# Softmax attention of one token over 8192 keys: longer chunks on VectorE, waits once per side, and the small steps between the pairs moved

## The chip, the core and the metric

The kernel runs on one NeuronCore of a Trainium2 chip. The core has five engines with their own instruction streams: TensorE (PE, matrix products), VectorE (DVE), ScalarE (ACT), GpSimd (POOL) and SyncE (SP, which here only issues transfers and waits), and 16 transfer (DMA) engines between device memory (HBM) and the on-chip memory (SBUF). Engines wait for one another by counting semaphores. The metric is the device time of one execution in microseconds; the median of three runs is taken.

## What is computed

One query row for each of 16 heads attends to 8192 keys of width 256, in bf16:

```python
B, H, Sq, Sk, D = 1, 16, 1, 8192, 256
def reference(q, k, v):
    scale = q.shape[-1] ** -0.5
    scores = jnp.einsum("bhqd,bhkd->bhqk", q, k) * scale
    p = _softmax(scores, axis=-1)
    return jnp.einsum("bhqk,bhkd->bhqd", p, v)
```

K and V are 67 MB each and every element is used once, so the kernel has to move 134 MB.

## The kernel before

**Tiling.** The 16 heads are taken as 8 pairs (`NP`). The K of a pair, "K h" below, fills 128 partitions with 64 for each head; a partition holds `J` = 128 keys, called columns, of 256 numbers each: 8.39 MB in all. V is laid out the same way. There are two buffers for K (`kbuf`, even and odd pairs) and one for V (`vbuf`). The columns of a pair are cut into two sides (`SIDES`) of 64.

**Scores.** Of the 64 columns of a side, GpSimd and ScalarE take the first 24 (`NPL`) and VectorE the other 40. GpSimd multiplies three columns at a time (a group, `GRP`) by the query and writes to `prod`, which holds two groups (L206 to L221); ScalarE adds each column up into `S` (L438 to L452). So GpSimd's group waits for the semaphore `sp`, with which ScalarE frees its half of `prod`, and ScalarE's for `tp`. A side has eight groups. VectorE multiplies and adds in one instruction per column (L243), in chunks of `CH` = 10 columns, four a side, and counts the chunks in `kd`. At the head of every chunk, and of every pair of groups on GpSimd, stand the same five waits: `k_waits` (the query of this pair has been copied, `qb`; K landed, `k0`, `k1`) and `side_wait` (`k6b`, `k7b`: the second sides of the last two Ks, which come as separate transfers).

**Softmax and V.** Behind each K VectorE takes the maximum over the columns (L263, semaphore `m`). TensorE turns it into a row (`turned`, L290), VectorE reduces that to one maximum per head (`xmax`, L231), TensorE spreads it (`spread`, L294), and ScalarE takes the exponentials (`expo`, L400 and L405, semaphore `ex`). TensorE then multiplies them with V, two columns at a time (`doubles`, L317), in a first half (semaphore `pa`) and a second, and adds up the sums (`total`, L305, semaphore `pr`). ScalarE copies the four strips of the result (`collect`, L419), called part rows here; TensorE adds these (`gather`, L339); VectorE takes the reciprocal of the sum (`recips`, L227), and ScalarE scales (`final`, L426).

**Where the small steps stand.** TensorE's loop does V of pair h-1 and then the maximum of pair h, in this order: wait `ex`, `doubles`, `total`, wait `m`, `turned`, wait `g`, `spread`, `keep_running` (a product with no use, L328), wait `cm`, `gather`, the query of pair h+2. VectorE and ScalarE do their small steps for earlier pairs between the columns of K h, at places written out by hand: `xmax` of pair h-1 behind the second chunk (20 columns) of side 0; `recips` of pair h-2 behind the first chunk of side 1; `expo` of pair h-1 behind group 4 of side 0 (the fifth), `collect` of pair h-2 behind group 6 of side 0, `final` of pair h-2 behind group 2 of side 1. Behind all 16 groups ScalarE copies the next query to `q_now` (`q_copy`, L396, semaphore `qb`).

**Transfers.** SyncE issues all of them in the order written out in `ORDER`, and stops at the first that can't go yet. K h waits until K h-2 is used up (`kd`, `tp`); V h until V h-1 is multiplied: a first half needs `pa`, a whole or a second half `pr`. The last Ks and Vs are cut: K6, K7 and V6 into halves ("k6", "k6+"), V7 at the columns 64, 92, 112 and 124 (`CUTS`). V7's first piece needs `pa` of V6, the later ones `pr` of V6. The columns of V7 from 92 on (`LAST_PAIRED`) are multiplied by 72 small products at the end (L382), and ScalarE and VectorE scale one half each of the last two rows (L472, L270).

```python
for kind, n, a, b, name in stream:
    if kind == "k" and n >= 2 and a == 0:
        sp.wait_ge(sem("kd"), (n - 1) * NC)
        sp.wait_ge(sem("tp"), (n - 1) * NG)
    elif kind == "v" and n >= 1 and a in (0, HJ):
        sp.wait_ge(*((sem("pa"), n) if b <= HJ else (sem("pr"), n + 2)))
```

## Time and profile before

| | us |
|---|---|
| median of three runs | 320.48 (320.45, 320.48, 321.91) |
| the profiled execution, whole time | 321.95 |
| its span, first to last instruction | 320.6 |
| VectorE busy | 229.2 (71%) |
| GpSimd busy | 210.8 (66%) |
| ScalarE busy | 195.3 (61%) |
| TensorE busy | 102.4 (32%) |
| moved from HBM | 134.23 MB, 419 GB/s over the span |

The profile is that of one execution. Its page has the busy time of each engine, the span in 40 slices with the busy tenths of each, the transfer queues, the chain of work that ended last, and the costliest groups of instructions. Other views list, in order of time, when instructions started, how long they took, and in brackets how long their engine had been idle and what ended that. A name with q behind it (SPq) is the engine's sequencer, which waits, branches and issues transfers. A group's line has the line of the code, the engine, the operation, the tile written and the ones read, the count, then the busy time in us, the mean of one in ns, and the idle time before it with its releaser.

### The profile page before, as it was taken

How to read it: one execution, taken by the hardware profiler on the slowest of the kernel's cores; microseconds unless marked ns; L12 is line 12 of the kernel's file. 1: busy time of each engine (PE TensorE's matmuls, PEld its weight loads, DVE VectorE, ACT ScalarE, POOL GpSimd, SP SyncE). 2: the span in 40 equal slices, each digit the busy share in tenths (PEclk: the TensorE clock that was granted, in tenths of full speed). 3: DMA queues.
4: the chain of work that ended last, by engine and by line, in shares of the span. 5: the costliest groups of instructions: out<-in, count | busy, mean ns of one | idle time of the engine just before them, and what ended most of it. 6: DMA issues, size and time to landing. Idle time of an engine off the chain costs nothing.

```text
span 320.6 us, 7869 instructions
## 1 busy us (share of the span) xinstructions
PE 102.4 (32%) x718; PEld 45.6 (14%) x718; DVE 229.2 (71%) x1305; ACT 195.3 (61%) x840; POOL 210.8 (66%) x146
## 2 busy tenths in 40 slices
PE   0000000037002570049102570027502104835678
PEld 0000000013000230014000230003200002412335
DVE  0008888688868888788878886788878886888810
ACT  2005766586656874777737873487757874788631
POOL 3008885879858685858658781769858785878400
PEclk9999999999655597557855596556955555978779
DMA  9999999999999999999999999999999999999994
GB/s 394 393 393 523 393 393 507 409 393 482 401 409 409 491 393 417 393 393 515 401 393 499 417 393 491 425 393 425 425 421 429 482 433 393 384 405 454 433 360 202
DMA packets 3353, 134.27 MB, mean 419 GB/s; under 512 B 374, under 2 KB 406, under 8 KB 662
## 3 DMA queue, kind: packets, MB, share of 16 engines
q1 hardware_dynamic: 3332, 134.23, 97.9%
q8 instruction: 1, 0.02, 0.0%
q14 instruction: 2, 0.02, 0.0%
q10 hardware_dynamic: 18, 0.01, 0.0%
HBM read 134.23 MB, written 0.01 MB: 419 GB/s over the span
## 4 chain that ended last, share of the span: by engine, by line
DMA 31%; DVE 25%; DVEq 21%; issue 18%; PE 3%; ACT 1%; SPq 0%
DMA kbuf<-in_k_dram 31%; DVE kbuf L243 25%; DVEq L243 13%; DVEq L156 2%; PE acc L317 2%; DVEq L238 2%; DVEq L152 1%; DVEq L157 1%; PE ob L382 1%; ACT E L405 0%; DVEq L254 0%; DVEq L257 0%; DVEq L237 0%; DVEq L153 0%; DVE small L231 0%
## 5 line engine op out<-in xcount | busy, mean ns | idle before, releaser
L243 DVE SCALAR_TENSOR_TENSOR kbuf<-kbuf,qrow x640 | 223.8, 417 | 75.0 <-issue 72.5
L214 POOL TENSOR_TENSOR prod<-kbuf,q_now 128x768 f32<-128x768 bf16 x128 | 208.0, 1639 | 88.0 <-issue 41.6
L445 ACT ACTIVATE prod<-prod x384 | 155.4, 405 | 105.7 <-POOL prod L214 92.0
L317 PE MATMUL acc<-vbuf,E 128*64 128x512 bf16 x494 | 70.0, 452 | 25.1 <-DMA vbuf<-in_v_dram 23.3
L445 ACT ACTIVATION_READ_ACCUMULATOR prod<-prod x384 | 71.6, 186 | 0.0
L243 DVE DVE_READ_ACCUMULATOR kbuf<-kbuf,qrow x640 | 52.9, 83 | 0.0
L317 PEld LDWEIGHTS acc<-vbuf,E 128*64 128x64 bf16 x494 | 31.9, 130 | 61.9 <-DMA vbuf<-in_v_dram 25.2
L290 PE MATMUL mx<-ident,small 128*1 128x128 f32 x16 | 4.3, 364 | 105.7 <-DVE small L263 105.7
L294 PE MATMUL mx<-small 1*64 1x1 f32 x32 | 2.8, 239 | 58.1 <-DVE small L231 58.1
L290 PEld LDWEIGHTS mx<-ident,small 128*1 128x1 f32 x16 | 0.7, 80 | 106.7 <-DVE small L263 106.7
L339 PE MATMUL ob<-comb,small 98*2 98x128 f32 x64 | 7.6, 386 | 24.8 <-ACT comb L419 24.8
L405 ACT ACTIVATE E<-S,negb 64x128 bf16 (+1 forms) x16 | 13.8, 865 | 1.4 <-ACT negb L400 1.2
L328 PE MATMUL spare<-ident 128*128 128x512 f32 x16 | 13.8, 955 | 0.0
L294 PEld LDWEIGHTS mx<-small 1*64 1x64 f32 x32 | 2.1, 183 | 61.7 <-DVE small L231 61.7
L419 ACT ACTIVATE comb<-acc 98x512 f32<-98x512 f32 x8 | 4.6, 579 | 6.4 <-PE tot L305 6.4
L339 PEld LDWEIGHTS ob<-comb,small 98*2 98x2 f32 x64 | 2.8, 101 | 36.0 <-ACT comb L419 34.2
L405 ACT ACTIVATION_READ_ACCUMULATOR E<-S,negb 64x1 f32 x16 | 7.9, 494 | 0.0
L227 DVE RECIPROCAL small<-tot 34x1 f32 (+1 forms) x8 | 1.2, 154 | 8.8 <-PE tot L305 8.8
L426 ACT ACTIVATE qo<-ob,small 2x128 f32 (+1 forms) x14 | 4.9, 353 | 0.1
L400 ACT ACTIVATE negb<-mx 128x1 f32<-128x1 f32 x8 | 1.3, 161 | 5.6 <-PE mx L294 5.6
L263 DVE TENSOR_REDUCE small<-S 128x1 f32 x8 | 2.3, 286 | 2.5 <-DVE kbuf L243 2.5
L281 PE MATMUL qrow<-qo,which 2*128 (+1 forms) x8 | 2.9, 393 | 2.9 <-DMA qo<-in_q_dram 2.6
(25 smaller groups left out, 22.0 us busy)
## 6 DMA issues: line engine op xcount, KB each, us to landing
kbuf<-in_k_dram SPq DMA_DIRECT2D x4, 4096.0 KB, 36.6
vbuf<-in_v_dram SPq DMA_DIRECT2D x3, 4096.0 KB, 14.4
vbuf<-in_v_dram SPq DMA_DIRECT2D x1, 1792.0 KB, 9.1
vbuf<-in_v_dram SPq DMA_DIRECT2D x1, 1280.0 KB, 11.9
vbuf<-in_v_dram SPq DMA_DIRECT2D x1, 768.0 KB, 13.3
vbuf<-in_v_dram SPq DMA_DIRECT2D x1, 256.0 KB, 13.5
kbuf<-in_k_dram SPq DMA_DIRECT2D x6, 31.9
vbuf<-in_v_dram SPq DMA_DIRECT2D x6, 28.8
```

What stands on the lines that cost most here:

```text
L156: e.wait_ge(sem("k6b"), (h * SIDES + s + 3) // (NP * SIDES) * 16 + 16)
L214: pool.tensor_tensor(out=prod[:, b * GRP * D : (b + 1) * GRP * D].rearrange("p (b d) -> p b d", b=GRP), in0=kbuf[:, ds(par * (J * D) + s * ...
L238: with dve.Fori(0, SC) as c:
L243: ins = dve.scalar_tensor_tensor(out=col, in0=col, scalar=SCALE, in1=qrow[:, ds(par * 512, D)], op0=ALU.mult, op1=ALU.mult, accum_out=S[:, ...
L290: pe.matmul(mx[0:1, 0:P], lhsT=m[:, :], rhs=ident[:, :], start=True, stop=True).then_inc(sem("mT"), 1)
L294: ins = pe.matmul(sm[n * HP : (n + 1) * HP, :], lhsT=ones[0:1, :].to_broadcast([1, HP]), rhs=g[:, n : n + 1], start=True, stop=True,)
L317: ins = pe.matmul(acc[at : at + STRIP, :], lhsT=E[:, x : x + STRIP], rhs=vbuf[:, j * D : (j + 2) * D], start=(j < 4), stop=(j >= J - 4), s ...
L328: pe.matmul(spare[:, :].rearrange("p (b x) -> p b x", x=P), lhsT=ident[:, :], rhs=ident[:, :].rearrange("p (b x) -> p b x", b=1).to_broadc ...
L339: ins = pe.matmul(ob[row : row + 2, 0:HW], lhsT=sel[:, 2 * n : 2 * n + 2], rhs=comb[:, n * D + a : n * D + a + HW], start=(n == 0), stop=( ...
L405: ins = act.activation(out=E[rows, 0 : 2 * J].rearrange("p (b two i t) -> p b i two t", b=J // BLK, two=2, t=2)[:, :, :, :, x], in_=S[rows ...
L426: ins = act.activation(out=qo[:, ds(i * D + a, HW)], in_=ob[row : row + 2, 0:HW], func=ACT.Copy, scale=recip[row : row + 2, ds(i, 1)],)
L445: ins = act.activation(out=part, in_=part, func=ACT.Copy, scale=SCALE, accum_out=S[:, ds(par * J + s * HJ + i * GRP + b, 1)],)
```

## The change

`CH` becomes 20, so VectorE has two chunks a side. The five waits are made once per side, ahead of the inner loop, on VectorE and on GpSimd, followed by a `nop` that counts up a semaphore `turn` that nobody waits for. The small steps move: `late` is 0 for pairs 0 to 6 and 1 for the last, and they stand in side `late`. On VectorE `xmax` and `recips` both come behind its first chunk (20 columns). On ScalarE `collect` comes behind group 1, `expo` behind group 3 and `final` behind group 6.

```diff
-CH = 10
+CH = 20
...
                 with pool.Fori(0, SIDES) as s:
+                    k_waits(pool, h)
+                    side_wait(pool, h, s)
+                    pool.nop().then_inc(sem("turn"), 1)
                     with pool.Fori(0, SG // 2) as i:
-                        k_waits(pool, h)
-                        side_wait(pool, h, s)
                         for b in range(2):
...
+                late = dve.snap(h // LAST)
                 with dve.Fori(0, SIDES) as s:
+                    k_waits(dve, h)
+                    side_wait(dve, h, s)
+                    dve.nop().then_inc(sem("turn"), 1)
                     with dve.Fori(0, SC) as c:
-                        k_waits(dve, h)
-                        side_wait(dve, h, s)
                         for b in range(CH):
...
                         ins.then_inc(sem("kd"), 1)
-                        with dve.If(s == 0):
-                            with dve.If(c == 1):
+                        with dve.If(c == 0):
+                            with dve.If(s == late):
                                 with dve.If(h > 0):
                                     xmax(h, 1)
-                        with dve.If(s == 1):
-                            with dve.If(c == 0):
                                 with dve.If(h > 1):
                                     recips(h, 2)
...
+                late = act.snap(h // LAST)
...
                         ins.then_inc(sem("sp"), 1)
-                        with act.If(s == 0):
-                            with act.If(i == 4):
+                        with act.If(s == late):
+                            with act.If(i == 1):
+                                with act.If(h > 1):
+                                    collect(h, 2)
+                            with act.If(i == 3):
                                 with act.If(h > 0):
                                     expo(h, 1)
                             with act.If(i == 6):
-                                with act.If(h > 1):
-                                    collect(h, 2)
-                        with act.If(s == 1):
-                            with act.If(i == 2):
                                 with act.If(h > 1):
                                     final(h, 2)
```

## The prediction

> **What bounds the kernel now.** I read the page's busy tenths first, then SyncE's waits, then the chain of waits and the timelines of single engines at the places that these name. K h and V h are the K and V of pair h; a full one is 8.39 MB.

> ```profile
> span 320.6 us, 7869 instructions
> DMA  9999999999999999999999999999999999999994
> SPq L137 <- PE tot L305: 113.0, 6, 27.5
> SPq L126 <- POOL prod L214: 105.2, 6, 50.9
> SPq L137 <- PE acc L317: 53.4, 2, 38.9
> 0.81 21.88 DMA kbuf<-in_k_dram
> 162.53 38.12 DMA kbuf<-in_k_dram
> ```

> The transfer engines are busy in every slice but the last, so the time is that of the stream of bytes, plus whatever empties the queue, plus the work behind the last byte. SyncE's rows say what can empty it: an issue of V stands behind TensorE (L305, or L317 for a half), one of K behind GpSimd and VectorE. No engine's speed counts by itself; what counts is whether it lets SyncE issue before the queue is dry.

> ```profile
> 268.54 9.74 PE L317 MATMUL acc<-vbuf,E 128*64 128x512 bf16 x64 [15.50 <-DMA vbuf<-in_v_dram]
> 287.96 5.12 PE L317 MATMUL acc<-vbuf,E 128*64 128x512 bf16 x32 [1.16 <-DMA vbuf<-in_v_dram]
> 297.68 5.33 PE L317 MATMUL acc<-vbuf,E 128*64 128x512 bf16 x32 [4.60 <-DMA vbuf<-in_v_dram]
> 78.33 0.33 SPq L137 DMA_DIRECT2D vbuf<-in_v_dram  x1
> 118.56 0.33 SPq L137 DMA_DIRECT2D vbuf<-in_v_dram  x1
> 153.25 0.33 SPq L137 DMA_DIRECT2D vbuf<-in_v_dram  x1
> ...
> 274.86 3.81 SPq L137 DMA_DIRECT2D vbuf<-in_v_dram  x2
> 293.12 0.33 SPq L137 DMA_DIRECT2D vbuf<-in_v_dram  x1
> 317.88 0.32 SPq L144 DMA_DIRECT2D out_dram<-qo  x1
> ```

> TensorE started V5, the front half of V6 and its back half as they landed. Between the first two lie two halves, 19.4 us; between the last two one half, 9.7 us. That is the stream undisturbed. K0 landed at 22.7 (0.81 + 21.88), so 2.5 us go to the start of a stream. At this rate K5, nine transfers on, would be in at 22.7 + 9 x 19.4 = 197.3; the chain has it at 162.53 + 38.12 = 200.65. So 3.35 us were lost before K5. The issues show where: V1 went out at 78.33, 2.6 us before K2 was due (80.9), and V2 at 118.56, 1.1 us before K3 was due (100.3 + 19.4 = 119.7). V3 at 153.25 had over 5 us. A start takes 2.5 us, so these two were late. The last bytes were in at 317.88 (L144 waits for them).

> **The change part by part.**

> VectorE's chunks:

> ```profile
> L243 DVE SCALAR_TENSOR_TENSOR kbuf<-kbuf,qrow x640 | 223.8, 417 | 75.0 <-issue 72.5
> 92.39 0.29 DVE L263 TENSOR_REDUCE small<-S 128x1 f32 x1 [0.31 <-DVE kbuf L243]
> 94.50 0.42 DVE L243 SCALAR_TENSOR_TENSOR kbuf<-kbuf,qrow  x1 [1.83 <-issue]
> 94.85 0.08 DVE L243 DVE_READ_ACCUMULATOR kbuf<-kbuf,qrow  x1
> 95.19 0.08 DVE L243 DVE_READ_ACCUMULATOR kbuf<-kbuf,qrow  x1
> L214 POOL TENSOR_TENSOR prod<-kbuf,q_now 128x768 f32<-128x768 bf16 x128 | 208.0, 1639 | 88.0 <-issue 41.6
> 201.62 3.24 POOL L214 TENSOR_TENSOR prod<-kbuf,q_now 128x768 f32<-128x768 bf16 x2 [7.87 <-DMA kbuf<-in_k_dram]
> 235.69 3.23 POOL L214 TENSOR_TENSOR prod<-kbuf,q_now 128x768 f32<-128x768 bf16 x2 [3.35 <-issue]
> 239.42 1.64 POOL L214 TENSOR_TENSOR prod<-kbuf,q_now 128x768 f32<-128x768 bf16 x1 [0.50 <-ACT prod L445]
> 269.74 3.23 POOL L214 TENSOR_TENSOR prod<-kbuf,q_now 128x768 f32<-128x768 bf16 x2 [3.35 <-issue]
> ```

> A column takes 0.34 us (94.85 to 95.19), a K's 80 take 27.3. The end of a K takes 0.31 + 0.29 + 1.83 = 2.4. VectorE's idle time put down to issue is 72.5 us: 24 before the first K, 1.83 at each of six starts, and the other 37 over 56 gaps between chunks, about 0.7 each. Seven gaps of a K become three. The two that disappear into a side cost from nothing to 0.7 each, the gap between sides 0.9; with 0.4 for the maximum and the reciprocal a K is 27.3 + 2.4 + 0.9 + 0.4 + (0 to 1.4), 31 to 32.4 us, where it was about 35. I take 31.5: 20 columns give the sequencer 6.8 us to run ahead.

> What is late next is the GpSimd-ScalarE loop. VectorE waits at each K for ScalarE's copy of q, made behind all 16 groups, and GpSimd's K starts stand 34.07 and 34.05 us apart (201.62, 235.69, 269.74). So a K costs 34.05, not 31.5.

> GpSimd's own waits: the gap before a pair of multiplies is 0.50 and its releaser is ScalarE's sum, two groups back. The five waits before it stand inside that time, while the second multiply runs, so moving them out gives nothing; a pair stays at 3.74 (235.69 to 239.42). If they were the gap, up to 0.34 a pair would go; I take 0 and keep 0.34 for a rival. The two added nops per K cost a semaphore update each, 0 to 0.3 us, hidden by the same loop on GpSimd and by the spare 2.5 us on VectorE.

> The moved steps in K1 to K6:

> ```profile
> 108.12 1.02 PE L339 MATMUL ob<-comb,small 98*2 98x128 f32 x8 [3.35 <-ACT comb L419]
> 109.40 9.10 PE L317 MATMUL acc<-vbuf,E 128*64 128x512 bf16 x64
> ```

> TensorE began V1 only behind the gather of V0's part rows, held 3.35 us by ScalarE's collect. The collect now comes ahead of the exponentials, and these one group (1.87 us) sooner. V1 then starts some 6 us earlier, at about 103.4, and V2's issue moves from 118.56 to about 112.5. For K1 only the exponentials move, some 1.9 us: V1's issue goes to about 76.5. Both are then ahead by more than the 2.5 us start, and K5 lands at 197.3. The collect and the reciprocal wait for the total of V(h-2); behind them stand ScalarE's groups and VectorE's next chunk. That total is out before K h starts (V1's at 118.5, and K3 is not in before 119.7), so nothing is held. None of these steps issues a transfer.

> The last K, which decides:

> ```profile
> 25.84 0.42 ACT L445 ACTIVATE prod<-prod  x1 [22.45 <-POOL prod L214]
> 46.13 0.42 ACT L445 ACTIVATE prod<-prod  x1 [0.29 <-issue]
> 280.47 0.17 ACT L400 ACTIVATE negb<-mx 128x1 f32<-128x1 f32 x1
> 281.70 0.87 ACT L405 ACTIVATE E<-S,negb 64x128 bf16 x1
> 285.15 0.57 ACT L419 ACTIVATE comb<-acc 98x512 f32<-98x512 f32 x1
> 316.81 2.18 PE L382 MATMUL ob<-vbuf,E 128*2 128x128 bf16 x72
> 319.04 0.36 ACT L472 ACTIVATE qo<-ob,small 2x128 bf16<-2x128 f32 x1 [3.01 <-PE ob L382]
> ```

> Pair 6's exponentials now stand in K7 behind 12 groups of ScalarE instead of 5. TensorE's V6 waits for them; V7's front half (L128, L137) waits for V6's front half; nothing else is left to issue. Before, they ended at 282.57, V6's front landed at 287.96, and V7 went out at 293.12, with V6's back half on its way until 297.68. Now:
> - K5 in at 197.3, GpSimd starts 0.97 later (201.62 - 200.65): 198.3. Two Ks of 34.05: K7 at 266.4.
> - In K0, where nothing interrupts, GpSimd starts at 23.8, ScalarE's first group at 25.84, its 12th at 46.13, ending 1.2 later: 23.5 us behind GpSimd's start. So 289.9; the collect of 0.57, partly in slack, adds 0.3: 290.2. The maximum is there: from a start near 267, VectorE's 60 columns take 20.5 and the gaps 1 to 2, about 289.
> - The exponentials, 280.47 to 282.57, 2.1; TensorE starts at 292.4.
> - V6's front half at the row of 287.96, 5.12: V7's front half is issued at 297.6 instead of 293.12.
> - V6's back half is in at 197.3 + 5 x 19.4 = 294.3. So the **queue runs dry** for about 5.5 us. From an empty queue a half takes 9.7 + 2.5 = 12.2: 309.8. (V6's front, issued at 274.86 as the queue ran out, took 13.1: the upper end.)
> - The last 64 columns: 9.7 undisturbed, 10.5 the other way (317.88 - 297.68 less 9.7). I take 10.0: 319.8.
> - From the last byte: 8 of the 72 small matmuls (72 take 2.2) 0.25, then as before from TensorE's end at 319.04 to the span's end at 320.6, 1.55. Span 321.6.

> Pair 7's exponentials follow V6's end, some 3.5 us behind 297.6, by a maximum and 2.1 us of ScalarE, about 305: before V7's front lands, so they cost nothing. Outside the span the execution has 321.95 - 320.6 = 1.35; so **323.0 us**, 1.0 above the profiled execution and 2.5 above the median of the three runs. Two of those were 1.5 shorter than the profiled execution, which fits a chance number of late issues; since the sum leaves none before K5, I carry no part of that difference over.

> The clock of TensorE in V6's front half:

> ```profile
> 290.00:291.00 1.00, 1.00 (x8) 0.42 (x6) 1.00 (x9) 0.95 (x6) 1.00 (x1) 0.51 0.45 197
> 291.00:292.00 1.00, 1.00 (x12) 0.53 (x10) 1.00 (x9) 0.20 (x1) 1.00 (x2) 1.00 1.14 492
> ```

> The windows view gives the granted clock behind the five engines, before the transfers' share: 0.51, then 1.00. V6's front half, from 287.96, so ran its first 3 us at half clock. At full clock it would cost what V5's back half did: V6 was issued at V5's middle, 274.86, and V5 ended at 278.28 (268.54 + 9.74), 3.4 us. [...]

> **The rivals.**
> [...]
> - **The hoisted waits do shorten GpSimd's pair** (the other side, faster): from 3.74 to 3.4. K6 and K7 up to group 12 are 14 pairs, 4.8 us; V7 goes out at 292.8, the dry stretch nearly closes, 305.0 + 10.0 + 1.8 + 1.35 = 318.2. It decides from 0.19 a pair (2.5 / 14). Against: the releaser is ScalarE.
> - **The chunks don't do what they say** (slower): the gaps stay, a K costs 35.2, K7 starts 2.3 later: 325.3. Or V1 or V2 is still late, up to 3.35 more: 326.3.

> **How the numbers follow.** Forecast 0.55, full clock 0.18, shorter pair 0.15, gaps stay 0.12. About 0.5%, 1.6 us, is what a measurement here can tell from no change: 318.9 to 322.1. Slower takes the forecast and the last rival, 0.66; same 0.20; faster 0.14. The range is 319.5 to 325.3: the forecast's bounds (13.1 for the half, 10.5 for the columns, 1.4 more) reach 325, the warm clock lies inside, most of the shorter pair and of a late V1 outside.

> **What would show it.** V2's issue near 112 and K5 used at about 198; K7 from GpSimd at 266; pair 6's exponentials ending at 292, V6's front following at once; SyncE's first V7 issue near 297.6 and the transfers' share falling before it. The prediction is wrong if that issue comes before 292, if GpSimd's gap falls under 0.3, or if K5 still lands at 200.

## The result, and the profile after

| | before | after |
|---|---|---|
| median, us | 320.72 (320.45 to 321.91, now 4 runs) | 325.51 (324.83 to 326.57, 4 runs) |
| profiled execution, us | 321.95 | 326.57 |
| its span, us | 320.6 | 325.2 |

After takes 1.0145 times as long as before (95% interval 1.0106 to 1.0184): slower, with the sign and by the mechanism of the forecast, but 2.5 us above its 323.0 and 0.2 above the end of its range. The profiled execution was the slowest of the four. The ratios, here and below, leave out executions more than 1.5% above the fastest of their kernel.

The page's rows of the span, of the busy share of the transfer engines in 40 slices and of the bytes they moved, after:

```profile
span 325.2 us, 7165 instructions
DMA  9899899899899999999998999989999999992994
GB/s 388 387 459 444 387 508 395 387 508 395 387 508 395 419 476 395 451 443 395 500 403 387 508 395 419 476 387 419 423 451 480 419 391 423 423 431 69 400 396 187
```

Before, only the last slice was short of a 9. Now there is a hole in the 37th slice (69 GB/s, 293 to 301 us). The 8s ahead of it cost nothing that the trace shows: K5 landed at 197.65 all the same (157.17 + 40.48 in the chain), against 197.3 for the undisturbed stream. Windows of 2 us in that stretch of after (busy time of TensorE, its weight loads, VectorE, ScalarE, GpSimd; then the granted clock of TensorE, the transfers' share, GB/s):

```profile
294.00:296.00 2.00, 1.69 (x8) 0.74 (x10) 2.00 (x13) 1.85 (x10) 0.13 (x2) 0.50 0.00 0
296.00:298.00 2.00, 2.00 (x16) 0.95 (x14) 1.49 (x10) 1.00 (x7) 2.00 (x2) 0.67 0.00 0
298.00:300.00 2.00, 2.00 (x22) 1.09 (x20) 0.00 (x0) 1.97 (x8) 1.15 (x1) 1.00 0.00 0
```

For six whole microseconds nothing moves, while TensorE, ScalarE and VectorE work. What starts the stream again is SyncE's issue of V7. SyncE's timeline of after:

```profile
76.99 0.33 SPq L137 DMA_DIRECT2D vbuf<-in_v_dram  x1
111.54 0.33 SPq L137 DMA_DIRECT2D vbuf<-in_v_dram  x1
...
299.46 0.33 SPq L137 DMA_DIRECT2D vbuf<-in_v_dram  x1
...
321.84 0.32 SPq L144 DMA_DIRECT2D out_dram<-qo  x1
```

V1 and V2 go out earlier than before, as meant; V7 goes out 6.3 us later (299.46 against 293.12). The chain to it, from the timelines of ScalarE and TensorE:

```profile
292.10 0.15 ACT L401 ACTIVATE negb<-mx 128x1 f32<-128x1 f32 x1
293.31 0.86 ACT L406 ACTIVATE E<-S,negb 64x128 bf16 x1
```

```profile
290.65 0.38 PE L295 MATMUL mx<-small 1*64 1x1 f32 x4 [15.49 <-DVE small L232]
290.96 2.08 PE L329 MATMUL spare<-ident 128*128 128x512 f32 x2
292.97 1.02 PE L340 MATMUL ob<-comb,small 98*2 98x128 f32 x8
294.31 8.56 PE L318 MATMUL acc<-vbuf,E 128*64 128x512 bf16 x64 [0.33 <-ACT E L406]
...
311.98 8.01 PE L318 MATMUL acc<-vbuf,E 128*64 128x512 bf16 x46 [6.52 <-DMA vbuf<-in_v_dram]
...
321.44 2.18 PE L383 MATMUL ob<-vbuf,E 128*2 128x128 bf16 x72
```

The spread of pair 6's maximum is out in time (290.65), so the exponentials stand only behind ScalarE's groups: they run from 292.10 (280.47 before). TensorE waits for them, no longer for V6, which had long landed, and its front half ends where V7 is issued. V7's products start 12.5 us behind that issue. GpSimd's starts of K5, K6 and K7, which set when ScalarE reaches its 12th group, and the next pair of K5:

```profile
198.77 3.22 POOL L215 TENSOR_TENSOR prod<-kbuf,q_now 128x768 f32<-128x768 bf16 x2 [6.84 <-issue]
202.50 1.64 POOL L215 TENSOR_TENSOR prod<-kbuf,q_now 128x768 f32<-128x768 bf16 x1 [0.50 <-ACT prod L447]
...
233.59 3.23 POOL L215 TENSOR_TENSOR prod<-kbuf,q_now 128x768 f32<-128x768 bf16 x2 [3.51 <-issue]
...
268.40 3.24 POOL L215 TENSOR_TENSOR prod<-kbuf,q_now 128x768 f32<-128x768 bf16 x2 [3.51 <-issue]
```

K5 starts 2.85 us earlier than before. But a K now takes 34.82 where it took 34.06 (the mean of 34.07 and 34.05), so K7 starts only 1.3 earlier. VectorE's two rows among the costliest groups:

```profile
L246 DVE SCALAR_TENSOR_TENSOR kbuf<-kbuf,qrow x640 | 220.3, 413 | 46.2 <-issue 46.2
...
L264 DVE TENSOR_REDUCE small<-S 128x1 f32 x8 | 2.3, 286 | 31.8 <-ACT prod L447 31.8
```

VectorE did get faster: its idle time put down to issue fell from 72.5 to 46.2 us. What it gained it spends waiting for ScalarE, 31.8 us over the eight maxima.

### The profile page after: what moved, and what is told of

The parts are those of the page before. It is cut to its first block, busy times and chain, and to the rows that moved or that the text cites. A ratio compares the mean times of both kernels' runs of the same rounds, so it can differ in the third digit from the quotient of the medians.

```text
span 325.2 us, 7165 instructions
## 1 busy us (share of the span) xinstructions
PE 103.9 (32%) x718; PEld 46.6 (14%) x718; DVE 224.9 (69%) x1305; ACT 195.3 (60%) x840; POOL 210.1 (65%) x146
## 4 chain that ended last, share of the span: by engine, by line
POOL 23%; DMA 23%; ACT 16%; issue 15%; ACTq 12%; PE 5%; POOLq 5%; SPq 0%
POOL prod L215 23%; DMA kbuf<-in_k_dram 19%; ACT prod L447 14%; ACTq L447 8%; PE acc L318 4%; DMA vbuf<-in_v_dram 4%; POOLq L215 3%; ACTq L443 2%; ACT E L406 1%; PE ob L383 1%; ACT q_now L397 1%; ACTq L456 1%; POOLq L212 0%; ACTq L459 0%; POOLq L214 0%
## 5 line engine op out<-in xcount | busy, mean ns | idle before, releaser
L215 POOL TENSOR_TENSOR prod<-kbuf,q_now 128x768 f32<-128x768 bf16 x128 | 207.3, 1639 | 87.0 <-issue 46.6
L246 DVE SCALAR_TENSOR_TENSOR kbuf<-kbuf,qrow x640 | 220.3, 413 | 46.2 <-issue 46.2
L318 PE MATMUL acc<-vbuf,E 128*64 128x512 bf16 x494 | 71.2, 459 | 44.5 <-DMA vbuf<-in_v_dram 42.4
L246 DVE DVE_READ_ACCUMULATOR kbuf<-kbuf,qrow x640 | 51.0, 80 | 0.0
L318 PEld LDWEIGHTS acc<-vbuf,E 128*64 128x64 bf16 x494 | 32.8, 132 | 81.5 <-DMA vbuf<-in_v_dram 43.8
L295 PE MATMUL mx<-small 1*64 1x1 f32 x32 | 2.9, 245 | 70.5 <-DVE small L232 70.5
L264 DVE TENSOR_REDUCE small<-S 128x1 f32 x8 | 2.3, 286 | 31.8 <-ACT prod L447 31.8
L329 PE MATMUL spare<-ident 128*128 128x512 f32 x16 | 14.7, 1018 | 0.0
L295 PEld LDWEIGHTS mx<-small 1*64 1x64 f32 x32 | 2.2, 191 | 74.1 <-DVE small L232 74.1
L340 PE MATMUL ob<-comb,small 98*2 98x128 f32 x64 | 7.3, 373 | 0.0
L340 PEld LDWEIGHTS ob<-comb,small 98*2 98x2 f32 x64 | 2.7, 99 | 11.5 <-issue 9.8
L329 PEld LDWEIGHTS spare<-ident 128*128 128x128 f32 x16 | 3.6, 282 | 0.1
```

Source lines behind the costliest of these rows:

```text
L215: pool.tensor_tensor(out=prod[:, b * GRP * D : (b + 1) * GRP * D].rearrange("p (b d) -> p b d", b=GRP), in0=kbuf[:, ds(par * (J * D) + s * ...
L246: ins = dve.scalar_tensor_tensor(out=col, in0=col, scalar=SCALE, in1=qrow[:, ds(par * 512, D)], op0=ALU.mult, op1=ALU.mult, accum_out=S[:, ...
L295: ins = pe.matmul(sm[n * HP : (n + 1) * HP, :], lhsT=ones[0:1, :].to_broadcast([1, HP]), rhs=g[:, n : n + 1], start=True, stop=True,)
L318: ins = pe.matmul(acc[at : at + STRIP, :], lhsT=E[:, x : x + STRIP], rhs=vbuf[:, j * D : (j + 2) * D], start=(j < 4), stop=(j >= J - 4), s ...
L329: pe.matmul(spare[:, :].rearrange("p (b x) -> p b x", x=P), lhsT=ident[:, :], rhs=ident[:, :].rearrange("p (b x) -> p b x", b=1).to_broadc ...
L340: ins = pe.matmul(ob[row : row + 2, 0:HW], lhsT=sel[:, 2 * n : 2 * n + 2], rhs=comb[:, n * D + a : n * D + a + HW], start=(n == 0), stop=( ...
```

## The experiments

The theory is that of the prediction: the late steps of the last K hold V7's issue until the queue is dry. Its rivals: the hoisted waits or the longer chunks cost the time; the tests and moved steps slow ScalarE in every K; TensorE's half clock costs the time. Each run is compared with before on its own chip.

| run | median, us (range, runs) | before beside it | ratio (95%) |
|---|---|---|---|
| e1 no late steps | 320.54 (319.69–322.05, 12) | 321.30 | 0.9969 (0.9944–0.9995) |
| e2 late steps alone | 341.20 (340.54–341.74, 4) | 321.30 | 1.0600 (1.0542–1.0658) |
| e3 chunks, waits alone | 320.57 (318.19–324.09, 12) | 321.30 | 0.9961 (0.9930–0.9991) |
| e4 `final` at its old place | 326.56 (325.34–328.12, 4) | 321.30 | 1.0166 (1.0109–1.0223) |
| e5 idle products before V7 | 327.27 (327.06–328.57, 4) | 321.13 | 1.0205 (1.0176–1.0233) |
| e6 V7 into K6's buffer | 319.69 (319.07–320.57, 12) | 321.13 | 0.9965 (0.9949–0.9980) |
| e7 chunks and waits undone | 327.01 (325.94–328.34, 4) | 321.13 | 1.0176 (1.0145–1.0207) |
| e8 idle products, two places | 326.44 (325.61–326.68, 4) | 321.31 | 1.0159 (1.0137–1.0182) |
| e9 the change again | 326.08 (325.27–326.64, 4) | 321.31 | 1.0145 (1.0116–1.0174) |
| e10 more, moved | 326.73 (325.78–327.09, 5) | 321.04 | 1.0179 (1.0166–1.0193) |
| e11 the change again | 325.36 (324.66–325.58, 4) | 321.04 | 1.0125 (1.0107–1.0142) |
| e12 idle products without a gap | 324.50 (324.09–324.91, 7) | 321.23 | 1.0089 (1.0055–1.0123) |

### e1: the change without its late steps

```diff
-                        with act.If(s == late):
+                        with act.If(s == 0):
...
-                            with dve.If(s == late):
+                            with dve.If(s == 0):
```

The two lines that compute `late` go as well.

> The changed kernel with late = 0 for every pair: the small steps stand in side 0 of the last K too. Theory (the late exponentials of pair 6 run the transfer queue dry): ScalarE's collect waits in K7 for V5's total at about 275, the exponentials of pair 6 end at about 281 to 282 instead of 294.2, V6's front half starts when it lands (about 286), V7's first piece is issued at about 291 instead of 299.5, the queue does not run dry, and the time falls by 5 us or more, to 318.5 to 320.5. Rival (the longer chunks, the waits per side or the early steps of K1 to K6 cost the time): it stays near 325.

The whole loss is gone: 320.5 us, 5 below the change. SyncE's issue of V7 (five issues grouped in one row) and TensorE's V6, in the timelines of e1:

```profile
291.35 11.77 SPq L137 DMA_DIRECT2D vbuf<-in_v_dram  x5
```

```profile
285.27 6.04 PE L317 MATMUL acc<-vbuf,E 128*64 128x512 bf16 x32 [7.64 <-DMA vbuf<-in_v_dram]
```

TensorE waits for V6 itself again, and V7 goes out at 291.35, 8.1 us before the change's. The page's transfer row of e1 has a 9 in every slice but the last. So the late side of the last K costs the 5 us, and the rest of the change gains a little at most (0.9969). The edit also takes the test against `late` out of every K, and K7 starts 0.6 us earlier for it (267.81 against 268.40); that is the smaller part of the 8.1.

### e2: the late steps alone, on the kernel before

```diff
-                        with act.If(s == 0):
-                            with act.If(i == 4):
+                        with act.If(s == late):
+                            with act.If(i == 4 - late):
...
-                            with act.If(i == 6):
+                            with act.If(i == 6 - 2 * late):
...
-                            with act.If(i == 2):
+                            with act.If(i == 2 + 4 * late):
```

VectorE's two steps move to side 1 of the last K in the same way, `recips` by `c == late`.

> The kernel before with one thing changed: in the last K the maximum, the reciprocal, the exponentials, the part rows and the final scaling stand in side 1 (behind its 20th column, and behind groups 3, 4 and 6). Theory: GpSimd starts K7 at 269.7 as before, ScalarE's 12th group ends 23.7 later, the exponentials end at about 295.6, V7's first piece is issued at about 301 instead of 293.1, and the time is 327 to 328.5, above the changed kernel, since K5 lands late as well. Rival (something else in the change costs the time): 320 to 321.5.

A miss: this edit confounds itself, and 341 us is far above the 5 us of e1. A group's first sum on ScalarE, first of the change, then of e2; GpSimd's starts and SyncE's V7 in e2:

```profile
202.58 0.42 ACT L447 ACTIVATE prod<-prod  x1 [0.48 <-issue]
```

```profile
209.36 0.42 ACT L447 ACTIVATE prod<-prod  x1 [0.84 <-issue]
```

```profile
205.18 3.23 POOL L214 TENSOR_TENSOR prod<-kbuf,q_now 128x768 f32<-128x768 bf16 x2 [3.57 <-issue]
...
241.70 3.23 POOL L214 TENSOR_TENSOR prod<-kbuf,q_now 128x768 f32<-128x768 bf16 x2 [3.58 <-DMA kbuf<-in_k_dram]
```

```profile
315.57 5.29 SPq L137 DMA_DIRECT2D vbuf<-in_v_dram  x5
```

In the side that holds the late steps the gap before a group's first sum is 0.84 us ahead of the second group (209.36) and 0.83 ahead of the third, both put down to issue; ahead of the second the change has 0.48. A K takes 36.5 us (205.18 to 241.70), K7 starts at 278.20, and V7 goes out at 315.57. That computing the places from `late` is the cause is an inference; it was not tried alone. There is a second difference: `collect` stands behind the exponentials here and not ahead of them, TensorE's gather waits for it, and V6's front half starts at 309.32, 31.1 us behind GpSimd's K7, where the change needs 25.9 (268.40 to 294.31). So this run can't separate the late steps from either; e1 does.

### e3: the chunks and the waits alone

```diff
-CH = 10
+CH = 20
...
+                    k_waits(pool, h)
+                    side_wait(pool, h, s)
+                    pool.nop().then_inc(sem("turn"), 1)
```

The same on VectorE; the small steps stay where they were, `xmax` behind the first chunk of 20.

> The kernel before with the chunks of 20 and the waits per side, the small steps left where they were (the maximum behind 20 columns of side 0, the reciprocal now behind 20 columns of side 1). Theory: VectorE's K falls from 35.2 to about 28 us of work plus a wait for ScalarE, GpSimd's loop stays at 34.1 to 34.3 a K, so the K before the last does not start earlier by more than what V1's issue gains; VectorE's last K ends with ScalarE's at about 302 instead of 305.2; 319 to 320.5. Rival (the hoisted waits shorten GpSimd's pair of 3.74): GpSimd's K under 33 and the time under 318.5. Rival (the chunks cost time): over 322.

By the ratio it is 0.4% faster than before, with an interval that just excludes 1. GpSimd's starts in e3:

```profile
200.80 3.23 POOL L215 TENSOR_TENSOR prod<-kbuf,q_now 128x768 f32<-128x768 bf16 x2 [7.86 <-issue]
...
234.99 3.22 POOL L215 TENSOR_TENSOR prod<-kbuf,q_now 128x768 f32<-128x768 bf16 x2 [3.51 <-issue]
```

A K takes 34.19, no less than before (34.06). The rival of the shorter pair falls: GpSimd's pace is not set by its five waits. The gap ahead of a K grew from 3.35 to 3.51; the nop stands there now.

### e7: the chunks and the waits undone, the late steps kept

The converse of e3, on the change; the waits go back on VectorE too, and `xmax` stands behind 20 columns as in the change.

```diff
-CH = 20
+CH = 10
...
-                    k_waits(pool, h)
-                    side_wait(pool, h, s)
-                    pool.nop().then_inc(sem("turn"), 1)
                     with pool.Fori(0, SG // 2) as i:
+                        k_waits(pool, h)
+                        side_wait(pool, h, s)
```

> The changed kernel with chunks of 10 and the five waits in every chunk and pair of groups again; all moved steps stay moved. Theory: the chunks and waits have no part in the loss: GpSimd's K takes 34.5 to 34.7 us (34.8 in the changed kernel, of which the waits per side with their nop are 0.15), the exponentials of pair 6 end at 294 to 295, V7's first piece is issued near 299.5, the time is 325 to 326.5. Rival (the longer chunks cost time): under 323.

GpSimd's starts, SyncE's V7, and the first products behind the maximum on TensorE, in e7:

```profile
199.02 3.23 POOL L214 TENSOR_TENSOR prod<-kbuf,q_now 128x768 f32<-128x768 bf16 x2 [7.13 <-DMA kbuf<-in_k_dram]
...
233.72 3.23 POOL L214 TENSOR_TENSOR prod<-kbuf,q_now 128x768 f32<-128x768 bf16 x2 [3.35 <-issue]
```

```profile
301.05 0.33 SPq L137 DMA_DIRECT2D vbuf<-in_v_dram  x1
```

```profile
292.52 0.37 PE L293 MATMUL mx<-small 1*64 1x1 f32 x4 [16.30 <-DVE small L231]
```

A K takes 34.70, so the chunks don't set it: ScalarE does, with the same late test as in the change. But the time lies 0.5 us above the range expected: V7 goes out 1.6 us later than in the change, because the late maximum now stands behind a slower VectorE: its row is spread at 292.52, where the change had it at 290.65. So once the maximum is late, VectorE's pace is on the chain as well, and the longer chunks keep it off; by the ratios this is worth some 1 us (1.0176 against 1.0145, their intervals overlap).

### e4: where a K's 0.8 us come from

```diff
-                            with act.If(i == 6):
+                        with act.If(s == 1):
+                            with act.If(i == 2 + 4 * late):
                                 with act.If(h > 1):
                                     final(h, 2)
```

> The changed kernel with the final scaling back in side 1 behind group 2 for K2 to K6 (the last K as in the change). Theory: the final behind group 6 of side 0 costs GpSimd's loop 0.5 to 0.6 us a K, because it follows the exponentials too closely to be absorbed; back at its old place a K costs 34.2 instead of 34.8, K7 starts 1 to 1.2 us earlier, and the time is 324.2 to 324.6. Rival (the exponentials behind group 3 or the nops make the K longer): GpSimd's K stays at 34.8 and the time at 325.3.

A miss: the K came to 34.70 and not 34.2 (GpSimd in e4):

```profile
233.41 3.23 POOL L215 TENSOR_TENSOR prod<-kbuf,q_now 128x768 f32<-128x768 bf16 x2 [3.74 <-issue]
...
268.11 3.23 POOL L215 TENSOR_TENSOR prod<-kbuf,q_now 128x768 f32<-128x768 bf16 x2 [3.74 <-issue]
```

But this does not clear `final`: the run tests a place computed from `late` in side 1, and the gap ahead of a K is 3.74 here and 3.51 in the change. Those 0.23 us come with the edit, and without them a K would be some 0.35 shorter than in the change. So this run leaves open what `final` at an early place costs. Set side by side, the starts of K5 and K6 stand apart by 34.07 (before), 34.19 (e3), 34.52 (e1) and 34.82 (the change). Chunks, waits and nop give 0.12; the steps at early places 0.33; the test against `late` instead of a constant 0.3. The last is the only difference between e1 and the change in these Ks, so it is shown; how the 0.33 divides among the three steps is open.

### e6: does the wait act through V6's buffer?

V7 goes into K6's buffer. Its issues wait for K6 to be used up instead of for V6's products; its products read `kbuf`. The late steps stay.

```diff
+                elif name == "w0":
+                    sp.wait_ge(sem("kd"), LAST * NC)
+                    sp.wait_ge(sem("tp"), LAST * NG)
...
-                if kind == "k":
-                    buf = kbuf[:, n % 2 * J * D :]
+                if kind == "k" or n == LAST:
+                    buf = kbuf[:, (n if kind == "k" else LAST - 1) % 2 * J * D :]
```

> The changed kernel, but V7 goes into the buffer of K6, so that its first piece waits for K6 to be used (265 us) and no longer for V6's front half; the late exponentials stay where they are. Theory (the late exponentials cost time only through V7's wait and the dry queue): V7 is issued at about 274 behind V6, the queue never runs dry, the last bytes are in at 314 to 315, TensorE follows pair 7's exponentials (about 306) with 6.5 + 1.6 + 2.2 us and becomes the end: 317.5 to 320, below the kernel before. Rival (the late steps cost time by themselves, by VectorE, ScalarE or TensorE being late): 323 or more.

In e6's timelines, SyncE's V7; ScalarE's second exponential of pair 6; TensorE's V7:

```profile
276.51 2.62 SPq L140 DMA_DIRECT2D kbuf<-in_v_dram  x5
```

```profile
294.04 0.86 ACT L413 ACTIVATE E<-S,negb 64x128 bf16 x1
```

```profile
307.62 5.45 PE L321 MATMUL acc<-kbuf,E 128*64 128x512 bf16 x46 [0.88 <-ACT E L413]
```

The exponentials are as late as in the change (294.04 against 293.31), and V6's front half too. But V7 was issued at 276.51, the stream never stops, and the time is 319.69 us, 5.8 below the change (by medians and by the ratios) and 0.35% below before. Late exponentials cost nothing by themselves; they cost through the one issue that waits for V6's buffer. Its median is the lowest of the kernels run here, but by the ratios e6, e3 and e1 (0.9965, 0.9961, 0.9969) can't be told apart.

### e5, e8, e10, e12: TensorE's half clock

In the change TensorE enters both V6's front half and V7 at half clock: 0.50 at 294.31 and at 311.98. Idle products (`keep_running`, of no use) are tried here as a means to keep the clock up.

```diff
+                    with pe.If(h == NP):
+                        for _ in range(5):
+                            keep_running()
                     pe.wait_ge(sem("v"), h * 16)
```

> The changed kernel with five more idle products on TensorE between the wait for pair 7's exponentials and the wait for V7 (V7's first piece landed 6 us behind those exponentials, so they cost no time of their own). Theory for the tail: in the changed kernel TensorE began V7 at half clock, 46 products took 8.0 us instead of 6.35, and TensorE instead of the last transfer ended late; at full clock they take about 5.8 with the wait for the second piece, the end follows the last transfer again, and the time is 1.2 to 1.6 us under the changed kernel, about 324.0 to 324.4. Rival (the tail is set by the transfers alone): no difference from the changed kernel, 325.3 to 326.

TensorE's V7 and SyncE's output issue (behind the last byte) in e5:

```profile
314.25 3.64 PE L318 MATMUL acc<-vbuf,E 128*64 128x512 bf16 x32 [1.34 <-DMA vbuf<-in_v_dram]
318.55 1.70 PE L318 MATMUL acc<-vbuf,E 128*64 128x512 bf16 x14 [0.65 <-DMA vbuf<-in_v_dram]
```

```profile
324.12 0.32 SPq L144 DMA_DIRECT2D out_dram<-qo  x1
```

V7's products now follow the bytes at full clock (1.00 in every window of 1 us from 308 to 324; two waits for DMA instead of one run of 8.01 us), and from the last byte to the span's end it is 326.2 - 324.1 = 2.1 us instead of 3.4. But the time went up, a miss: in this profile K7 starts 0.7 us later than in the change (269.07), V6 1.0 later (295.27), its front half takes 6.5 us instead of 5.1, most of it at half clock (0.50 until 301.06), and V7 goes out at 301.79. Whether the idle products have a part in that, this run does not show. e8 adds 15 calls (two records each) behind pair 6's maximum:

```diff
                     turned()
+                    with pe.If(h == LAST - 1):
+                        for _ in range(15):
+                            keep_running()
```

> The changed kernel with idle products on TensorE at both places where it waits in the last K: fifteen ahead of the wait for pair 6's maximum (TensorE is idle there from 275 to 290) and the five ahead of V7 of the run before. Theory (with the queue dry, TensorE's half clock lies on the path twice, in V6's front half and in V7): V6's front half takes 3.4 to 3.7 us instead of 5.1 to 6.5, V7's first piece is issued at 297.7 to 298.5, V7's 46 products take 5.3 to 5.5 instead of 8.0, the span's tail behind the last byte is 2.1 instead of 3.4; the time is 2.5 to 3.5 us under the changed kernel run beside it. Rival (the clock lies off the path): no difference.

TensorE in e8, and the window in which its clock fell:

```profile
275.52 13.14 PE L329 MATMUL spare<-ident 128*128 128x512 f32 x30
291.06 0.38 PE L295 MATMUL mx<-small 1*64 1x1 f32 x4 [2.39 <-DVE small L232]
```

```profile
290.00:291.00 1.00, 0.00 (x0) 0.00 (x0) 1.00 (x8) 0.84 (x5) 0.73 (x1) 0.97 1.14 492
291.00:292.00 1.00, 0.94 (x5) 0.80 (x6) 1.00 (x6) 0.69 (x3) 0.77 (x1) 0.50 0.69 295
```

The products ended at 288.66; 2.3 us later the clock fell (290.94), and V6, from 295.01, ran at 0.50 until 297.78, as it did until 297.32 in the change. The gain expected did not come; there is no difference in time from e9, the change beside it, that is clear of the intervals:

> The changed kernel once more, on the chip of the run with the clock kept, as its measure: 325 to 326.6, V6's front half 5.1 to 6.5 us by where the clock comes up, the tail behind the last byte 3.4.

e10 takes 17 calls there and, instead of the five, six ahead of TensorE's wait for the exponentials:

```diff
+                    with pe.If(h == NP):
+                        for _ in range(6):
+                            keep_running()
                     pe.wait_ge(sem("ex"), h)
```

> [...] If TensorE's half clock has the price that the traces show, V6's front half takes 3.4 us instead of 4.9 to 6.5, V7 goes out at 297.5 to 298.5, and the tail is 2.1 instead of 3.4: about 2.5 us below the change beside it, 323.5. If the clock falls all the same while the small steps of 291 to 294 run, only the tail is shorter: 324.8. If the tail's gain is illusory too, as the times of e5 and e8 suggest, the same as the change within 0.5 us.

> The change as it is, beside e10_warm_both on the same chip: 325.3 to 326.6 in all theories.

e10 is slower than the change beside it (326.73 against 325.36), which none of the three expectations had. The profiles don't show why: their spans are 324.5 and 324.3, and that of e10 is its fastest execution, that of e11 its slowest. The cause of this 1.4 us stays open. TensorE and the clock in e10:

```profile
294.77 8.78 PE L318 MATMUL acc<-vbuf,E 128*64 128x512 bf16 x64 [1.81 <-ACT E L412]
```

```profile
294.00:295.00 1.00, 0.23 (x2) 0.14 (x4) 1.00 (x7) 0.97 (x4) 0.50 (x1) 0.97 0.08 33
298.00:299.00 1.00, 1.00 (x10) 0.55 (x8) 0.00 (x0) 0.59 (x3) 1.00 (x2) 0.82 0.00 0
```

The clock lasted through the small steps (1.00 in every window from 286 to 294), then fell, after a gap of 1.81 us, just as V6 began: a mean of 0.97 is full clock for 0.94 of that window, so at 294.94. It came back at 298.36. e12 fills that gap too:

```diff
+                    with pe.If(h == LAST):
+                        for _ in range(2):
+                            keep_running()
```

> As e10_warm_both, with two more idle products ahead of the wait for pair 6's exponentials, where TensorE of e10 was idle for 1.81 us and the clock fell at 294.97, just behind the start of V6. If the half clock of V6's front half has the price that the traces show, that half now takes 3.4 to 3.8 us instead of 5.2, V7 goes out at about 298.3 instead of 300.1 and the span is 1.5 to 1.8 shorter than e10's 324.5: about 324 to 325 us beside the 326.7 of e10 and the 325.4 of the change. If idle products cost time in a way that the traces do not show (e10's other four executions took 326.7 to 327.1), 326.5 or more.

TensorE and SyncE in e12:

```profile
293.29 1.98 PE L329 MATMUL spare<-ident 128*128 128x512 f32 x4
295.21 7.10 PE L318 MATMUL acc<-vbuf,E 128*64 128x512 bf16 x64
```

```profile
298.89 5.31 SPq L137 DMA_DIRECT2D vbuf<-in_v_dram  x5
321.34 0.32 SPq L144 DMA_DIRECT2D out_dram<-qo  x1
```

Now V6's front half goes at full clock throughout (1.00 in every window from 290 to 304): 3.7 us from 295.21 to the issue at 298.89, where e10 took 5.4 (294.77 to 300.13). The tail is 323.4 - 321.3 = 2.1. The time is 324.50 us, and the interval of its ratio lies wholly below e10's: two calls more, four idle products, are worth about 2.2 us by the medians and 2.9 by the ratios, since the two ran on different chips. The profiles show 1.2 of it in the issue of V7. So V6's half clock is part of the price of the late steps. Against the change the gain is smaller and not certain, about 1.2 us by the ratios of e11 and e12 (their intervals overlap); K7 starts 0.6 later in e12 than in e11 (269.24 against 268.63). All four kernels with the added branches in TensorE's loop start K7 between 268.80 and 269.24, the three profiles of the change between 268.19 and 268.63; that the branches do it was not tried alone.

## Why the prediction was right in kind and short in size

- **VectorE's chunks.** Right: the gaps inside a side are gone, VectorE waits for ScalarE, and a K is set by the GpSimd-ScalarE loop. The rival of the gaps that stay fell.
- **GpSimd's pair.** Right: 3.73 from 198.77 to the next pair at 202.50 in the change (3.74 given). The rival of the shorter pair fell with e3. Its sum was short: K5, K6 and K7 up to the 12th group are 22 pairs and not 14, which would have been 7.5 us.
- **V1, V2 and K5.** Right in kind: V1 at 76.99 (76.5 given), V2 at 111.54 (112.5), and K5 used from 198.77 (198.3): 0.45 over.
- **"So a K costs 34.05".** Here the working failed. I costed one moved step, the collect, at 0.3 in K7 ("partly in slack"), and the steps and the new test in the two Ks before it at nothing. ScalarE has no slack there: its steps and tests are part of the loop that sets the K (0.33 and 0.3 by e3, e1 and the change), and the nops, which I took to be hidden, come with the other 0.12 of e3. Measured 34.82, so 0.76 too little for each of two Ks, 1.5 in all. K7 came at 268.40 and not 266.4.
- **Twelve groups to the exponentials.** Right: 23.7 behind GpSimd's start (292.10 - 268.40), 23.8 given.
- **V6's front half at 5.12.** Right: 294.31 to the issue at 299.46, the clock at 0.50 for its first 3 us. That the short products ahead of it would leave the clock there was my estimate, and no run shows it as a rule; in this trace they took 3.3 us (290.65 to 293.99) at 0.50, and the clock rose at 297.32. And that the half clock lasted 3.0 us, as before, is luck: the front half took 4.4 us in e11, 4.9 in e9 and 6.5 in e5, by where the clock came up (296.06, 296.66 and 301.06). The full clock, given 0.18, did not occur by itself; e12, with idle products in the gaps, had it (1.00, 3.7 us).
- **The dry queue.** Right: no transfer from 294 to 300. The first half landed 12.5 us behind its issue (311.98; 12.2 given), the rest 9.9 later (321.84; 10.0 given). The upper end of 13.1 was misread: when V6 was issued at 274.86 the queue was not empty, since K7's second half, behind V5 (in at 268.54), was due only at 278.2.
- **"From the last byte 1.8".** The other term that failed: it was 325.2 - 321.84 = 3.4. I carried over an end in which TensorE keeps up with the bytes. But the dry queue left TensorE idle for 6.52 us, from 305.5 to 311.98, its clock fell to 0.50 (at 307.56), and its 46 products for V7 took 8.01 us, so that the 72 small ones ended at 323.62 (321.44 + 2.18), 1.8 us behind the last byte. e5 and e12, with the clock kept at 1.00, have 2.1. So a second cost of the empty queue was left out: 1.55 us in this profile (the tail is 2.9 to 3.4 over the profiles of the change). Its size varied: e4, with the same idle time and no idle products, has a tail of 2.0, since its clock rose 2.7 us behind V7's first product (312.19 to 314.86) and not 5.8.

The misses are 0.45 + 1.5 + 0.3 + 1.55 = 3.8, less 0.1 in the twelve groups and 0.1 in the last columns: the 3.6 between the span of 321.6 given and the 325.2 measured; against the median the miss is 2.5. The range held 13.1 for the half and 10.5 for the columns, which did not come, but a K of 34.05 without a bound, and a tail without one. Those 1.4 us above the forecast also reach only 324.4, not 325; the end of the range, 325.3, was that of the rival in which the gaps stay.

## What to carry to other kernels

When the transfers are the bound, find the one buffer release on which the next issue hangs, and let no step on its chain slip behind other work, or give the load another buffer (e6): the same late steps then cost nothing (319.69 us against 321.13 for before). Count every step and every test that moves onto the engine that sets the pace of the loop; here it had no slack to hide them, and they cost 0.3 us a round. A queue that ran dry cost twice here, once as lost stream (no transfer from 294 to 300 us) and again as a TensorE whose clock fell while it waited (a tail of 3.4 us, where e5 has 2.1).

## What the runs showed of the hardware

```profile
293.00:294.00 1.00, 0.99 (x9) 0.33 (x8) 1.00 (x7) 0.98 (x4) 1.00 (x1) 0.50 0.16 66
297.00:298.00 1.00, 1.00 (x12) 0.45 (x10) 0.49 (x4) 0.05 (x1) 1.00 (x2) 0.84 0.00 0
307.00:308.00 1.00, 0.00 (x0) 0.00 (x0) 0.00 (x0) 0.00 (x0) 0.00 (x0) 0.78 1.14 492
317.00:318.00 1.00, 1.00 (x8) 0.48 (x6) 0.00 (x0) 0.00 (x0) 0.00 (x0) 0.60 0.99 420
```

A mean of 0.84 is 0.68 us of full clock and 0.32 of half, so it rose at 297.32; likewise it fell at 307.56 and rose at 317.80. These stand 10.24 us apart, three times 3.41. The two of e10 (294.94 and 298.36) are 3.42 apart. In before it changed at 290.98, 297.82, 301.22, 308.06 and 311.46, steps of 6.84 and 3.40; in e1 at 300.40, 303.82 and 310.64 (3.42, 6.82), in e4 at 297.78, 308.02 and 314.86 (10.24, 6.84), in e7 at 299.02 and 309.26 (10.24). How long a stretch ran at half clock differed: V7 from 311.98 to 317.80 in the change and from 312.19 to 314.86 in e4, V6 from 294.31 to 297.32 in the change and from 294.57 to 296.06 in e11. The clock fell 2.1 us after TensorE's last product before V7 (305.5 to 307.56) and after a gap of 1.8 in e10. In the 3.41 us ahead of the fall at 307.56 TensorE was busy for about 0.4 of the time (304.15 to 305.5). The busy time in the records did not by itself decide when it rose: the 3.42 us from 290.49 to 293.91 were 95% busy with the small f32 products (L295, L329, L340) and the clock stayed at 0.50; the next 3.41 were 90% busy, nearly all of it with V6's products, and at their end the clock rose. What makes it rise or fall is open.

**A test against `late` took ScalarE longer here than one against a constant.** A K took 0.3 us more with `s == late` than with `s == 0` (34.82 in the change, 34.52 in e1); ahead of the fourth group of the side with the small steps the gap put down to issue is 0.47 us in the change (206.32, 241.13) and 0.38 in e1 (277.70). With places computed from `late` it was 0.84 ahead of the second group (e2).
